# A backward pass of attention and MLP on one core: wq's gradient stored in one piece per block, the held-back stores moved behind the last V load, w2's gradient made first, and w3's gradient shared with ScalarE

## The chip, the cores and the metric

The kernel runs on one core of a Trainium2 chip. The metric is device time in microseconds. Before the change three executions took 749.34, 750.81 and 750.61 us, so the median is 750.61 us. The profiled execution took 750.92 us, of which its instructions span 749.1 us.

## The reference

A decode step with one token. The normalised row goes through attention over a cache of 32 heads with 8192 positions of 128 elements, and through a gated MLP (640 to 1728 to 640), and both are added to the input. The function returns that output and the gradients of eight inputs for a given output gradient.

```python
x = A_x
xn = _layernorm(x, axis=-1)
return x + _A_ref(xn, A_k_cache, A_v_cache, A_wq, A_wo) + _B_ref(xn, B_w1, B_w3, B_w2)
...
_out, _vjp = jax.vjp(_f, A_x, A_k_cache, A_v_cache, A_wq, A_wo, B_w1, B_w3, B_w2)
```

The K and V caches are each 64 MiB in bf16, and so are their gradients: each head loads 2 MiB of K and 2 MiB of V and stores as much in gradients. The gradients of the four attention and MLP weights are outer products of a row and a column: each is made by scaling one vector with a per-partition number.

## The kernel before

One head is one iteration of the main loop over `h`, 32 in all; four heads are a group `g` (eight groups), and two groups are a block `b` of wq (four blocks). In an iteration VectorE makes products of K with q and of V with the output gradient (`product`, L336), TensorE sums them through an identity matrix, and softmax and its gradient follow on small tiles. The gradients of V and K are four tiles `ot` of 1 MiB per head (`outer`): VectorE writes 24 of 32 rows of each (L345), ScalarE the other 8 (L349), and GpSimd's queue stores it (L351). Tiles of `ot` come from a pool of seven buffers; at the start the same seven hold the three parts of w2 (`w2c`), `diag` and `bc_sb`.

All loads go through SyncE's queue (SP) and nearly all stores through GpSimd's queue (POOL). VectorE, ScalarE, SP and POOL run their instructions in the order of the program; TensorE's order is set by the planner that builds the program. A wait at the head of SP or POOL holds all that is queued behind it. K has three buffers, which at the start hold w1, w3 and K of head 0. So `load_k(1)` must wait until the gradient of w1, made in place, has been stored, and `load_k(2)` until that of w3 has.

`mlp_steps` is a generator that is advanced between other pieces of work. Its order before the change: the forward part, `w2_grad(0)`, `dx_part(0)`, `w_grad` of w1; then, outside, `prep_steps(0)` (queries and output gradients of group 0: `qs_g` L258, five copies `woT` L248, `do_g` L274, all ScalarE); then `w2_grad(1)`, `w2_grad(2)`, `dx_part(1)`; the first S products of head 0; `w_grad` of w3; the rest of head 0's preparation. After that come `load_k(1)` and `load_k(2)` and the main loop.

`finish_steps(g)` makes the gradients of wo and wq of a finished group in four pieces, taken at the four calls of `gap()` in the next iteration. When the second group of a block is done it stores the block's wq gradient in five stores, one per 128 rows (`ci`), each behind the ScalarE instruction that makes it. Stores marked `later` go on the list `late`: those of wo of group 6, of wq of block 2 (five), and of wq of group 6. The list is stored at the head of iteration 30 (`h == H - 2`).

Of the kernel before, what the change touches and what calls it, by code (L numbers as in the profile page):

```python
# [11 lines left out]
ALU = mybir.AluOpType  # L12
ACTF = mybir.ActivationFunctionType
# [3 lines left out]
P = 128  # L17
# [4 lines left out]
def kernel(  # L22
# [22 lines left out]
    nc = tc.nc  # L45
    H = A_k_cache.shape[1]
    SK = A_k_cache.shape[2]
    DH = A_k_cache.shape[3]
    D = A_x.shape[2]
    F = B_w1.shape[1]  # L50
    assert DH == P and D % P == 0 and SK % (2 * P) == 0
    NC = D // P
# [4 lines left out]
    NG = H // GH  # L57
    ORDERED = {mybir.EngineType.DVE, mybir.EngineType.SP, mybir.EngineType.Pool, mybir.EngineType.Activation}
    GW = 8
    HB = GW // GH  # L60
# [4 lines left out]
    scale = float(DH) ** -0.5  # L65
# [21 lines left out]
    dwq_v = out_4.rearrange("(p ci) n -> p ci n", ci=NC)  # L87
# [4 lines left out]
    dw1_v = out_6.rearrange("(p ci) f -> p ci f", ci=NC)  # L92
    dw3_v = out_7.rearrange("(p ci) f -> p ci f", ci=NC)
# [3 lines left out]
    with tc.manual_schedule(engines=ORDERED):  # L97
# [8 lines left out]
        def load_k(h):  # L106
            Kt = kpool.tile([P, J, DH], BF16, name="Kt", tag="K")
            nc.sync.dma_start(Kt[:], kc[h])
            kv_tiles[h] = kv_tiles.get(h, [None, None])
            kv_tiles[h][0] = Kt  # L110

        def load_v(h):
            Vt = vpool.tile([P, J, DH], BF16, name="Vt", tag="V")
            nc.sync.dma_start(Vt[:], vc[h])
            kv_tiles[h] = kv_tiles.get(h, [None, None])
            kv_tiles[h][1] = Vt

        grp = {}
        late = []

        def store(dst, src, later=False):
            if later:
                late.append((dst, src))
            else:
                nc.gpsimd.dma_start(dst, src)
# [15 lines left out]
        w1t = kpool.tile([P, NC, F], BF16, name="w1t", tag="K")  # L141
        w3t = kpool.tile([P, NC, F], BF16, name="w3t", tag="K")
# [53 lines left out]
        xn_col = consts.tile([P, NC], F32, name="xn_col")  # L196
        xn_col_bf = consts.tile([P, NC], BF16, name="xn_col_bf")
        xn2 = consts.tile([P, NC, 2], BF16, name="xn2")
# [80 lines left out]
        def finish_steps(g):  # L279
            G_ = grp[g]  # L280
            wo_g = G_["wo"]
            on = small.tile([P, GH], F32, name="on")
            nc.scalar.copy(on[:], G_["on_ps"])
            on_bf = small.tile([P, GH], BF16, name="on_bf")
            nc.scalar.copy(on_bf[:], on[:])
            for r in range(GH):
                for ci in range(NC):
                    nc.tensor.matmul(accbank[:, OUT0 + ci:OUT0 + ci + 1], lhsT=wo_g[:, r, ci * P:(ci + 1) * P],
                                     rhs=on_bf[:, r:r + 1], start=False, stop=True, skip_group_check=True)
            for r in range(GH):  # L290
                nc.scalar.activation(wo_g[:, r, :], g_bc_bf[:], ACTF.Copy, scale=on[:, r:r + 1])
                if r == 1:
                    yield
            store(dwo_v[g], wo_g[:], g == NG - 2)
            yield
            b, k = divmod(g, HB)
            for ci in range(NC):
                nc.scalar.activation(G_["wq"][:, ci, :], G_["dqbc"][:].rearrange("p h d -> p (h d)"),
                                     ACTF.Copy, scale=xn_col[:, ci:ci + 1])
                if g < NG - HB and k == HB - 1:  # L300
                    store(dwq_v[:, ci, b * GW * DH:(b + 1) * GW * DH], G_["wq_all"][:, ci, :], g == NG - HB - 1)
                if ci == 2:
                    yield
            if g >= NG - HB:
                store(dwq_v[:, :, g * GH * DH:(g + 1) * GH * DH], G_["wq"], g < NG - 1)
            grp.pop(g)
# [7 lines left out]
        def new_head(h):  # L314
            st = Head()
            st.g, st.hh = divmod(h, GH)
            st.G = grp[st.g]
            st.K, st.V = kv_tiles.pop(h)
            hs[h] = st
            return st  # L320
# [89 lines left out]
        def keep_wq(st):  # L410
            st.wqT = small.tile([P, D], BF16, name="wqT", bufs=1)
            nc.scalar.copy(st.wqT[:], st.ps_wqT[:])
# [30 lines left out]
        def mlp_steps():  # L443
# [46 lines left out]
            bc_sb = opool.tile([P, 2, F], BF16, name="bc_sb", tag="o")  # L490
            for wi in range(2):
# [4 lines left out]
                for k, b0 in enumerate(range(0, NB, 4)):  # L496
# [6 lines left out]
                    src = bc_ps[:].rearrange("p b a -> p (b a)")[:, 0:cols]  # L503
# [8 lines left out]
            def w2_grad(k):  # L512
                b0, nb, nfull, w2c = w2_parts[k]
                for b, rows in blocks[b0:b0 + nb]:
                    for ci in range(NC):
                        nc.tensor.matmul(accbank[:, OUT0 + ci:OUT0 + ci + 1], lhsT=w2c[0:rows, b - b0, ci * P:(ci + 1) * P],
                                         rhs=hcol_bf[0:rows, b:b + 1], start=False, stop=True, skip_group_check=True)
                    nc.scalar.activation(w2c[0:rows, b - b0, :], g_bc_bf[0:rows, :], ACTF.Copy, scale=hcol[0:rows, b:b + 1])
                nc.gpsimd.dma_start(dw2_v[:, b0:b0 + nfull, :], w2c[:, 0:nfull, :])
                if nfull < nb:  # L520
                    nc.gpsimd.dma_start(out_8[NF * P:F, :], w2c[0:REST, nfull, :])
# [3 lines left out]
            def dx_part(wi, wt):  # L525
                for c0 in range(0, NC, 2):
                    n = min(2, NC - c0)
                    T = tpool.tile([P, n, F], BF16, name="T13", tag="T")
                    nc.vector.tensor_tensor(T[:], wt[:, c0:c0 + n, :],
                                            bc_sb[:, wi, :].unsqueeze(1).to_broadcast([P, n, F]), ALU.mult)  # L530
                    for i in range(F // DR1):
                        nc.tensor.matmul(dx_ps[:, c0:c0 + n, :], lhsT=ident_bf[:], rhs=T[:, :, DR1 * i:DR1 * (i + 1)],  # L532
                                         start=(wi == 0 and i == 0), stop=(wi == 1 and i == F // DR1 - 1),
                                         skip_group_check=True)

            def w_grad(wi, wt, dst):
                nc.vector.tensor_tensor(wt[:].rearrange("p c (a b) -> p c a b", b=2),  # L537
                                        bc_sb[:, wi, :].rearrange("p (a b) -> p a b", b=2).unsqueeze(1)
                                        .to_broadcast([P, NC, F // 2, 2]),
                                        xn2[:].unsqueeze(2).to_broadcast([P, NC, F // 2, 2]), ALU.mult)  # L540
                nc.gpsimd.dma_start(dst, wt[:])

            w2_grad(0)
            dx_part(0, w1t)
            w_grad(0, w1t, dw1_v)
            yield
            w2_grad(1)
            w2_grad(2)
            dx_part(1, w3t)
            yield  # L550
            w_grad(1, w3t, dw3_v)
            yield
            nc.vector.tensor_reduce(dxn_mlp[:], dx_ps[:], AX.X, ALU.add)

# [3 lines left out]
        def gap():  # L558
            if steps and next(steps[0], "end") == "end":
                steps.pop(0)  # L560
# [12 lines left out]
        exps(first)  # L573
        product(first, "DP", 1)
        next(mlp, None)
        load_k(1)
        load_k(2)
        prev = None
        for h in range(H):
            n = new_head(h + 1) if h + 1 < H else None  # L580
            c = hs.pop(h)
            g, hh = divmod(h, GH)
            if h == H - 2:
                for dst, src in late:
                    store(dst, src)
            if n:
                product(n, "S", 0)
            probs(c)
            outer(c, c.do, c.P2, c.Pf, dvc, h, 0)
            if prev:  # L590
                keep_dq(prev)
            gap()
            row_dots(c)
            attend(c)
            turn_wq(c)
            if n:
                product(n, "S", 1)
            outer(c, c.do, c.P2, c.Pf, dvc, h, 1)
            if h + 2 < H:
                load_v(h + 2)  # L600
            gap()
            dscores(c)
            outer(c, c.q, c.U2, c.Uf, dkc, h, 0)
            keep_wq(c)
            if n:
                row_max(n)
                product(n, "DP", 0)
            outer(c, c.q, c.U2, c.Uf, dkc, h, 1)
            if h + 3 < H:
                load_k(h + 3)  # L610
            gap()
            if n:
                exps(n)
                product(n, "DP", 1)
            weights(c)
            gap()
            if hh == 0 and g + 1 < NG:
                if (g + 1) % HB == 0:
                    load_wq((g + 1) // HB)
                load_wo(g + 1)  # L620
            if hh == 1 and g + 1 < NG:
                steps.append(prep_steps(g + 1))
                gap()
            if hh == 2:
                gap()
            prev = c
# [61 lines left out]
```

## Time and profile before

| what | value |
|---|---|
| median of three executions | 750.61 us |
| profiled execution, and its span | 750.92 us, 749.1 us |
| bytes read and written | 151.34 MB and 151.34 MB, 404 GB/s over the span |
| VectorE, TensorE, ScalarE, GpSimd busy | 84%, 73%, 63%, 12% |
| chain that ended last | DMA 61%, VectorE 28%, TensorE 6% |
| five stores of one wq block | 256 KB each, 20.3 us from issue to landing (median) |
| `ot` stores | 128 of 1024 KB, 29.0 us from issue to landing (median) |

The profile shows one execution. In the page's second part the span is cut in 40 slices, and a digit is a busy share in tenths. A row of windows gives, for each engine, the busy time and the instructions in a stretch, then TensorE's granted clock, the share of the 16 DMA engines that was busy, and GB/s. A row of the timeline gives start, duration, engine, line, the tile written and read, and in brackets the idle time before it with what ended it.

### The profile page before, as it was taken

What the parts mean: (1) busy time and instruction counts of PE and PEld (TensorE: products, weight loads), DVE (VectorE), ACT (ScalarE), POOL (GpSimd) and SP (SyncE); (2) the same over time, 40 slices, a digit from 0 to 9 for tenths busy, and PEclk for the clock granted to TensorE, in tenths of its full rate; (3) what the DMA queues carried; (4) which work ended last, traced back from release to release, by engine and by line L of the source; (5) the groups of instructions that cost most, each with busy time, mean ns of one, the idle gap of its engine ahead of it and who ended that gap; (6) DMA issues with size and microseconds to landing.
All of it is one profiled execution on the core that took longest, in us unless ns stands there. A gap on an engine that the chain in (4) does not pass through costs nothing.

```text
span 749.1 us, 15938 instructions
## 1 busy us (share of the span) xinstructions
PE 546.1 (73%) x6513; PEld 323.6 (43%) x6513; DVE 631.8 (84%) x709; ACT 473.3 (63%) x1419; POOL 88.0 (12%) x168
## 2 busy tenths in 40 slices
PE   5677798885868784887778772887787768677860
PEld 3453455452534452444444441444454435344440
DVE  5589999999779985999698993999698998899970
ACT  2453667685658752795666862787555966676772
POOL 0010111010011110111010120111101101101220
PEclk9597779777967887877788887778695989777765
DMA  9978999999999999999999999999999999999796
GB/s 341 415 281 326 421 427 426 422 424 427 425 433 422 422 419 425 426 423 418 431 426 425 425 380 425 426 428 420 429 429 423 429 415 430 427 424 425 311 367 197
DMA packets 37223, 303.71 MB, mean 405 GB/s; under 512 B 4012, under 2 KB 5742, under 8 KB 12062
## 3 DMA queue, kind: packets, MB, share of 16 engines
q0 software_dynamic: 21920, 151.35, 48.8%
q1 hardware_dynamic: 15218, 151.35, 48.5%
q8 instruction: 51, 0.84, 0.4%
q14 instruction: 22, 0.18, 0.1%
q10 hardware_dynamic: 12, 0.00, 0.0%
HBM read 151.34 MB, written 151.34 MB: 404 GB/s over the span
## 4 chain that ended last, share of the span: by engine, by line
DMA 61%; DVE 28%; PE 6%; issue 2%; ACT 1%; SPq 0%; POOL 0%; POOLq 0%; DVEq 0%; ACTq 0%
DMA out_dram<-ot 44%; DVE T L336 12%; DVE ot L345 11%; DMA out_dram<-wo_g 11%; DMA wo_g<-in_A_wo_dram 4%; DMA w3t<-in_B_w_dram 2%; PE psS L338 2%; PE dx_ps L532 1%; DVE S_sb L355 1%; DVE DP_sb L389 1%; DVE w3t L537 1%; PE ps_t L243 1%; PE psDP L338 0%; DVE P L374 0%; ACT woT L248 0%
## 5 line engine op out<-in xcount | busy, mean ns | idle before, releaser
L338 PE MATMUL psDP<-T,ident_bf 128*128 128x512 bf16 x512 | 181.3, 515 | 63.6 <-DVE T L336 63.6
L338 PEld LDWEIGHTS <-ident_bf 128*128 128x128 bf16 x1024 | 119.8, 119 | 213.7 <-issue 157.7
L349 ACT ACTIVATE ot<-qs_g,Uf 128x128 bf16<-128x128 bf16 x512 | 156.4, 389 | 66.5 <-DMA out_dram<-ot 56.4
L349 ACT ACTIVATE ot<-do_g,Pf 128x128 bf16<-128x128 bf16 x512 | 156.3, 389 | 17.7 <-DMA out_dram<-ot 16.8
L336 DVE TENSOR_TENSOR T<-Kt,qs_g 128x4096 bf16<-128x4096 bf16 x64 | 146.4, 2289 | 1.5 <-PE psDP L338 0.7
L338 PE MATMUL psS<-T,ident_bf 128*128 128x512 bf16 x512 | 143.3, 430 | 4.5 <-DVE T L336 4.4
L336 DVE TENSOR_TENSOR T<-Vt,do_g 128x4096 bf16<-128x4096 bf16 x64 | 145.9, 2280 | 0.0
L345 DVE TENSOR_TENSOR ot<-qs_g,U 128x3072 bf16<-128x3072 bf16 x64 | 112.2, 1753 | 38.6 <-DMA out_dram<-ot 38.4
L351 POOL DMA_DIRECT2D out_dram<-ot x128 | 68.2, 533 | 540.0 <-ACT ot L349 204.9
L345 DVE TENSOR_TENSOR ot<-do_g,P 128x3072 bf16<-128x3072 bf16 x64 | 112.3, 1755 | 5.6 <-DMA out_dram<-ot 4.7
L402 PEld LDWEIGHTS <-Kt 128*128 128x128 bf16 x2048 | 57.5, 98 | 13.7 <-issue 11.6
L402 PE MATMUL ob<-U,Kt 128*128 128x1 bf16 x2048 | 57.1, 164 | 3.2 <-DVE U L397 3.1
L382 PEld LDWEIGHTS <-Vt 128*128 128x128 bf16 x2048 | 57.4, 98 | 0.0
L382 PE MATMUL ob<-P,Vt 128*128 128x1 bf16 x2048 | 57.1, 163 | 0.0
L248 ACT COPY woT<-ps_t 128x512 bf16<-128x512 bf16 x40 | 23.0, 576 | 28.8 <-PE ps_t L243 28.6
L368 PEld LDWEIGHTS sm<-rsum,ones_f 128*128 128x128 f32 x64 | 15.8, 271 | 55.5 <-ACT E L367 50.8
L421 ACT ACTIVATE dq_diag<-ident_bf,odq 128x128 bf16<-128x128 bf16 x32 | 12.8, 399 | 40.5 <-DVE odq L417 40.5
L359 PE MATMUL sm<-ident_f,mrow 128*128 128x128 f32 x64 | 18.9, 387 | 26.0 <-DVE mrow L357 26.0
L376 ACT ACTIVATE Pf<-E,rZ 128x16 f32<-128x16 f32 x32 | 9.8, 307 | 38.4 <-DVE rZ L372 38.2
L367 ACT ACTIVATE E<-S_sb,negM 128x64 f32<-128x64 f32 x32 | 11.0, 343 | 33.8 <-DVE negM L364 33.7
L265 PE MATMUL ps_d<-woT,G_rep 128*128 128x512 bf16 x40 | 16.3, 408 | 21.9 <-ACT woT L248 21.7
L243 PE MATMUL ps_t<-ident_bf,wo_g 128*128 128x128 bf16 x160 | 16.9, 233 | 20.2 <-DMA wo_g<-in_A_wo_dram 18.4
(149 smaller groups left out, 522.6 us busy)
## 6 DMA issues: line engine op xcount, KB each, us to landing
out_dram<-ot POOLq DMA_DIRECT2D x128, 1024.0 KB, 29.0
Kt<-in_A_k_cache_dram SPq DMA_DIRECT2D x32, 2048.0 KB, 17.0
Vt<-in_A_v_cache_dram SPq DMA_DIRECT2D x32, 2048.0 KB, 13.9
wq_g<-in_A_wq_dram SPq DMA_DIRECT2D x4, 1280.0 KB, 28.7
wo_g<-in_A_wo_dram SPq DMA_DIRECT2D x8, 640.0 KB, 8.3
out_dram<-wo_g POOLq DMA_DIRECT2D x8, 640.0 KB, 24.3
out_dram<-wq_g POOLq DMA_DIRECT2D x15, 256.0 KB, 20.3
w1t<-in_B_w_dram SPq DMA_DIRECT2D x1, 2160.0 KB, 11.8
```

What stands on the lines that cost most here:

```text
L243: nc.tensor.transpose(ps_t[:, hh * DH:(hh + 1) * DH], wo_g[:, hh, ci * P:(ci + 1) * P], ident_bf[:])
L248: nc.scalar.copy(woT[:], ps_t[:])
L265: nc.tensor.matmul(ps_d[:], lhsT=G_rep[:, ci, :], rhs=woT[:], start=(ci == 0), stop=(ci == NC - 1))
L336: nc.vector.tensor_tensor(T[:], src[:, :, ds_], vec[:, ds_].unsqueeze(1).to_broadcast([P, J, DHH]), ALU.mult)
L338: nc.tensor.matmul(ps[:], lhsT=ident_bf[:], rhs=T[:, :, RUN * i:RUN * (i + 1)], start=(half == 0 and i == 0), stop=(half == 1 and i == DHH ...
L345: nc.vector.tensor_tensor(ot[:, 0:JD], vec.rearrange("p (a b) -> p a b", b=2).unsqueeze(1).to_broadcast([P, JD, DH // 2, 2]), w2[:, j0:j0 ...
L349: nc.scalar.activation(ot[:, j].rearrange("p a b -> p (a b)"), vec, ACTF.Copy, scale=wf[:, half, j - JD:j - JD + 1])
L351: nc.gpsimd.dma_start(dst[h][:, j0:j0 + JH, :], ot[:].rearrange("p j a b -> p j (a b)"))
L359: nc.tensor.matmul(st.sm[:, 8:8 + P], lhsT=mrow[:].to_broadcast([P, P]), rhs=ident_f[:], start=True, stop=True, skip_group_check=True)
L368: nc.tensor.matmul(st.sm[:, 3:4], lhsT=ones_f[:], rhs=rsum[:], start=True, stop=True, skip_group_check=True)
L382: mm = nc.tensor.matmul(st.ob[:, 0:1], lhsT=st.V[:, j, :], rhs=st.P2[:, j, 0:1], start=(j == 0), stop=(j == J - 1), skip_group_check=True)
L402: nc.tensor.matmul(st.ob[:, 1:2], lhsT=st.K[:, j, :], rhs=st.U2[:, j, 0:1], start=(j == 0), stop=(j == J - 1), skip_group_check=True)
```

## The change

Four edits:

- A block's wq gradient goes out in one store of 1280 KB when all five columns are made, in place of five stores of 256 KB.
- The list `late` is stored in iteration 29, right behind `load_v(31)`, in place of the head of iteration 30. It holds three stores in place of seven.
- `w2_grad(1)` moves ahead of `w_grad` of w1 and `w2_grad(2)` right behind it, both ahead of `prep_steps(0)`. `load_k(1)` and `load_k(2)` are called inside `mlp_steps`.
- For w3, ScalarE makes columns 3 and 4 of the gradient (two instructions of 1728 elements) and VectorE's one instruction makes columns 0 to 2.

```diff
             for ci in range(NC):
                 nc.scalar.activation(G_["wq"][:, ci, :], ...)
-                if g < NG - HB and k == HB - 1:
-                    store(dwq_v[:, ci, b * GW * DH:(b + 1) * GW * DH], G_["wq_all"][:, ci, :], g == NG - HB - 1)
                 if ci == 2:
                     yield
+            if g < NG - HB and k == HB - 1:
+                store(dwq_v[:, :, b * GW * DH:(b + 1) * GW * DH], G_["wq_all"][:], g == NG - HB - 1)
...
-            def w_grad(wi, wt, dst):
-                nc.vector.tensor_tensor(wt[:].rearrange("p c (a b) -> p c a b", b=2),
+            def w_grad(wi, wt, dst, nd):
+                for ci in range(nd, NC):
+                    nc.scalar.activation(wt[:, ci, :], bc_sb[:, wi, :], ACTF.Copy, scale=xn_col[:, ci:ci + 1])
+                nc.vector.tensor_tensor(wt[:, 0:nd].rearrange("p c (a b) -> p c a b", b=2),
...
             w2_grad(0)
             dx_part(0, w1t)
-            w_grad(0, w1t, dw1_v)
+            w2_grad(1)
+            w_grad(0, w1t, dw1_v, NC)
+            w2_grad(2)
+            load_k(1)
             yield
-            w2_grad(1)
-            w2_grad(2)
             dx_part(1, w3t)
             yield
-            w_grad(1, w3t, dw3_v)
+            w_grad(1, w3t, dw3_v, NC - 2)
+            load_k(2)
             yield
...
         next(mlp, None)
-        load_k(1)
-        load_k(2)
...
-            if h == H - 2:
-                for dst, src in late:
-                    store(dst, src)
...
             if h + 2 < H:
                 load_v(h + 2)
+            if h == H - 3:
+                for dst, src in late:
+                    store(dst, src)
             gap()
```

More of the change, by code (lines that the diff above doesn't have):

```diff
@@ L534, in dx_part @@
                                          skip_group_check=True)
-            def w_grad(wi, wt, dst):
-                nc.vector.tensor_tensor(wt[:].rearrange("p c (a b) -> p c a b", b=2),
+            def w_grad(wi, wt, dst, nd):
+                for ci in range(nd, NC):
+                    nc.scalar.activation(wt[:, ci, :], bc_sb[:, wi, :], ACTF.Copy, scale=xn_col[:, ci:ci + 1])
+                nc.vector.tensor_tensor(wt[:, 0:nd].rearrange("p c (a b) -> p c a b", b=2),
                                         bc_sb[:, wi, :].rearrange("p (a b) -> p a b", b=2).unsqueeze(1)
-                                        .to_broadcast([P, NC, F // 2, 2]),
-                                        xn2[:].unsqueeze(2).to_broadcast([P, NC, F // 2, 2]), ALU.mult)
+                                        .to_broadcast([P, nd, F // 2, 2]),
+                                        xn2[:, 0:nd].unsqueeze(2).to_broadcast([P, nd, F // 2, 2]), ALU.mult)
                 nc.gpsimd.dma_start(dst, wt[:])
```

## The prediction

> **What bounds the kernel now.** I read the page's slices first, then windows of 2 us over both ends, then the waits of SP, and last the timelines of ScalarE and POOL around the edits. The page:
>
> ```profile
> DMA  9978999999999999999999999999999999999796
> GB/s 341 415 281 326 421 427 426 422 424 427 425 433 422 422 419 425 426 423 418 431 426 425 425 380 425 426 428 420 429 429 423 429 415 430 427 424 425 311 367 197
> ```
>
> From slice 5 to 37 the DMA engines are full at about 425 GB/s; 303.7 MB at that rate are 715 us of the 749. What is left to win is the holes: slices 3 and 4, slice 24, and the end. Windows of the two large ones (last column GB/s):
>
> ```profile
> 42.00:44.00 2.00, 1.28 (x11) 0.64 (x10) 2.00 (x2) 0.95 (x3) 0.55 (x1) 1.00 0.70 281
> ...
> 48.00:50.00 2.00, 1.68 (x31) 1.56 (x29) 1.52 (x2) 2.00 (x3) 0.00 (x0) 1.00 0.09 35
> 50.00:52.00 2.00, 0.92 (x5) 0.45 (x5) 2.00 (x2) 2.00 (x4) 0.14 (x1) 1.00 0.00 0
> ...
> 66.00:68.00 2.00, 2.00 (x11) 0.90 (x10) 1.86 (x4) 0.99 (x4) 0.00 (x0) 1.00 0.35 147
> ...
> 706.00:708.00 2.00, 1.95 (x55) 1.47 (x53) 1.97 (x4) 1.08 (x4) 0.50 (x1) 1.00 0.43 168
> 708.00:710.00 2.00, 0.96 (x21) 0.70 (x19) 1.97 (x4) 2.00 (x7) 0.54 (x1) 1.00 0.13 53
> ```
>
> Summing what the eighteen windows from 40 to 76 lack against 425 gives 4.6 MB, 10.7 us. The seven from 702 to 716 lack 2.8 MB, 6.6 us. SP's waits between 40 and 80 us name the first hole's cause:
>
> ```profile
> SPq L108 <- DMA out_dram<-w1t: 35.0, 1, 35.0
> SPq L108 <- DMA out_dram<-w3t: 16.7, 1, 16.7
> ```
>
> K of head 1 is issued at 51.27, when w1's gradient has landed, and K of head 2 at 68.4, when w3's has. Meanwhile ScalarE (first rows) and POOL (last rows) show w2's stores coming after the first hole:
>
> ```profile
> 31.87 4.42 ACT L518 ACTIVATE w2c<-g_bc_bf,sm_f 128x640 bf16<-128x640 bf16 x6
> 40.66 0.60 ACT L258 ACTIVATE qs_g<-ps_q 128x512 bf16<-128x512 f32 x1 [4.38 <-PE ps_q L253]
> ...
> 47.17 5.84 ACT L518 ACTIVATE w2c<-g_bc_bf,sm_f 128x640 bf16<-128x640 bf16 x8
> ...
> 42.11 0.55 POOL L541 DMA_DIRECT2D out_dram<-w1t  x1 [4.53 <-DVE w1t L537]
> 51.86 1.40 POOL L519 DMA_DIRECT2D out_dram<-w2c  x2 [9.21 <-ACT w2c L518]
> ```
>
> The second hole is of another kind. POOL's rows there:
>
> ```profile
> 705.96 0.54 POOL L125 DMA_DIRECT2D out_dram<-wq_g  x1 [2.28 <-DMA out_dram<-ot]
> 708.71 0.54 POOL L125 DMA_DIRECT2D out_dram<-wo_g  x1 [2.21 <-DMA out_dram<-ot]
> 711.26 0.84 POOL L125 DMA_DIRECT2D out_dram<-wq_g  x1 [2.01 <-DMA out_dram<-ot]
> 714.03 2.48 POOL L351 DMA_DIRECT2D out_dram<-ot  x4 [1.92 <-ACT E L367]
> ```
>
> POOL's stores take eight semaphores in turn, so each waits until the one eight places ahead has landed. Landings keep coming every 2.5 to 2.8 us although 53 GB/s are moved, an eighth of the full rate. So not all 16 engines are at work: one of them is behind. The trace's records of semaphore increments say so: of the sixteen for one store fifteen had come by 706.0 and the last at 714.7, and the last ones follow one another every 2.5 us from 698 to 736. That engine has no hole here; it carries 1 MB of `ot` (64 KB its share) in 2.5 us, as when all run. The hole belongs to the other fifteen.
>
> **The change part by part.**
>
> **w2 first.** Two kinds of cost: ScalarE's order and the DMA queues.
>
> ScalarE: eight instructions of 0.73 us (5.84 / 8) move from 47.17 to 36.29, the end of the first six. There the engine is idle for 4.38 us, which holds six of them; TensorE had read all of w2 by 33.0, so none waits. The other two push `qs_g` and what follows by 1.5 us, `do_g` from 46.12 to 47.6. Head 0's first product on VectorE (48.73) waits for TensorE's sums of w3, which ran behind `ps_d` (last 45.70). At worst it comes 1.5 us later; at best, if the planner puts those sums earlier, VectorE's own gaps of 1.66 and 0.48 us there close and it comes 2.1 earlier.
>
> POOL: the store of w2's second part (0.98 MB) is issued at about 41, ahead of w1's gradient, which is ready at 41.8, so POOL does not hold that up. The queue does: 2.3 us more at 425 GB/s, less what 40 to 44 lacked (0.46 MB, 1.1 us). w1's gradient lands 1.2 us later and SP issues K of head 1 at 52.5. From there to K of head 2 the trace has 17.15 us, in which K (2.10 MB), w2 (1.23) and w3's gradient (2.21) are moved: 13.0 us at 425, and 4.1 of latency and gaps. Without w2 it is 10.1 plus 3.5 to 4.1 (some of the gaps, 0.85 us from 54 to 60, came as w2's stores started). So K of head 2 is issued between 66.1 and 66.7, some 2 us sooner than 68.4.
>
> Behind that point the queues are full until 700, so what the full stretch starts earlier the end is earlier. The other count: 1.23 MB moved into idle DMA time is 2.9 us, the most this part can give; nothing is its least. I take 2.2.
>
> **w3 shared.** VectorE 4.65 us × 3/5 = 2.79, so 1.86 us less on its chain, which is unbroken from 53 to 151. ScalarE's rate from 128 elements (0.306 us, eight of L349 in 2.45) and 640 (0.73): (0.73 − 0.306) / 512 per element, so 1728 take 1.63 us and two take 3.3. They lie in the 8.07 us that ScalarE waits before 61.08, and cost nothing; without that cover they would be 3.3 us on head 0. With the 1.5 us above, w3's gradient is ready at 57.4 at worst, before K of head 1 has gone through (about 59.5). The DMA order so decides, not VectorE: worth 0.3 us, between 0 and 1.
>
> **load_k inside the MLP.** SP has no other DMA between the old place and the new. Both loads wait for the same landings. Nothing.
>
> **One store per block.** Eight POOL instructions of 0.54 us fewer in blocks 0 and 1, beside a POOL busy 12%. A wq store now starts behind the fifth column in place of the first. At slice 24 the five small ones held POOL's eight places with few bytes and the rate was 380; that hole, (425 − 380) × 18.7 us = 0.84 MB or 2.0 us, is of the fifteen engines again. Between 0 and 2.0 gained, and 0.5 lost if the later start leaves a gap. I take 0.
>
> The Trainium skill (DMA: Bandwidth & Descriptors, Anatomy of one DMA) gives each such DMA about 2 us of fixed cost. By it the four fewer at the end would save up to 8 us. Here the slow engine's increments for the five small stores come 0.65 us apart, which is just their bytes: no fixed cost on the path.
>
> **Held-back stores earlier.** 2.62 MB go into POOL's order ahead of head 29's last two `ot`, just behind `load_v(31)` (684.65). The bytes ahead of the slow engine's end are the same; it has work throughout, so it ends when it did. Gained is a bubble of 0.4 us: after the last held-back store, 719.9 in the increments, the next 1 MB took 3.0 us in place of 2.55, as POOL had issued it late. Waiting behind: POOL issues head 29's last two when their places come free, some 7 us later than 690.42 and 695.51, and they land 6.2 us later (2.62 MB / 425). Who waits: VectorE's and ScalarE's tiles of head 31, seven buffers on. The second (718.97) needs what landed at 711.0, the third (721.11) what landed at 713.5: 8.0 and 7.6 us of slack, 1.8 and 1.4 left. Between 0.9 lost and 3.5 gained (rival one); I take 0.4 gained.
>
> The sum against the profiled execution of 750.9: −2.2 − 0.3 − 0 − 0.4 = −2.9, 748.0. The median of the runs is 0.3 below that execution, so 747.7.
>
> [...]
>
> **The rivals.**
>
> One: the end hole fills too. If the fifteen and the one share the work differently once POOL is not stopped by small stores, the end comes as early as the last store allows: issued at 735.16 it landed at 745.8 by the increments; with the least landing time of any `ot` store, 7.1 us, it would be 742.3. So 3.5 us more: 744.2. For it: 53 GB/s at 708. Against it: the increments every 2.5 us.
>
> Two: the gain at the start is eaten. K of head 1 comes 1.2 us later at least; if w1's gradient lands 3 us later, as its last engine was 2.1 us behind the rest already (49.0 and 51.1), and head 0 starts 1.5 later, the full stretch starts where it did, and only the 0.4 at the end is left: 750.2. For it: VectorE's chain from 53 to 151 has no gap. Against: DMA is full there as well.
>
> Three, slower: the held-back stores delay the last head. Stores landed between 7.1 and 39.1 us after issue. If the load of V 31 (2.1 MB, 5 us) goes ahead of them on the slow engine in place of beside them, head 29's tiles land 5 us later than I say, 1.4 to 1.8 of that is slack, and VectorE's last chain and all behind it moves 3.4; with rival two's lost start that is 747.7 + 2.5 + 3.4 = 753.6. It decides from 1.4 us on. For it: head 31's fourth tile already waits for its buffer (to 722.96). Against: before, the same load had landed by 697.6.
>
> **How the numbers follow.** The forecast 0.58 (its own range 746 to 749.1), rival one 0.14, two 0.16, three 0.12. Measured runs spread over 0.2%, 1.5 us, so faster means below 749.1: forecast and rival one, 0.72; the same is rival two, 0.16; slower is three, 0.12. The range from 743.2 (rival one with 1 us of slice 24) to 751.0 leaves out three and the ends of the others.
>
> **What would show it.** Right: two `w2c` groups of ScalarE joined from 31.9 to about 42; 42 to 44 near 400 GB/s; K of head 2 issued near 66.4; `w3t` on VectorE 2.8 us; in the last 50 us three L125 stores ahead of head 29's last `ot`, and still a stretch with less than half the rate. Wrong: no such stretch and an end before 742; SP's first L108 wait ending past 54; VectorE idle for `ot` after 715; slice 24 filled and the time lower by it.

## The result, and the profile after

The changed kernel takes 748.74 us (median of seven; 747.63 to 750.51) against 750.93 us before (median of seven). The two medians are 2.2 us apart. The ratio over all the runs is 0.9978, with a 95% interval from 0.9968 to 0.9988, and this is what the text goes by. Measured once more, with twelve runs, the ratio was 0.9979 (0.9967 to 0.9990). So the kernel is faster by 0.22%, some 1.7 us (0.9 to 2.4), which is just over what a measurement of this kernel can tell from no change. Its profiled execution took 749.1 us, with a span of 747.3 us.

The page of the changed kernel, second part:

```profile
DMA  9988999999999999999999999999999999999993
GB/s 341 413 318 330 405 428 422 423 419 426 425 429 427 422 423 422 426 420 421 431 428 424 424 419 424 408 431 418 431 425 427 427 401 427 426 426 411 414 384 109
```

Three of the holes have changed. Slice 3 went from 281 to 318 GB/s, slice 24 from 380 to 419, and the hole in the third slice from the end (311) has gone. In its place the last slice is emptier: 109 where it was 197. Windows of the changed kernel, with columns as in the prediction:

```profile
42.00:44.00 2.00, 0.31 (x3) 0.28 (x3) 2.00 (x2) 0.97 (x3) 1.66 (x3) 0.74 0.89 330
44.00:46.00 2.00, 2.00 (x14) 1.57 (x12) 1.51 (x1) 0.56 (x1) 0.00 (x0) 0.50 1.18 443
...
50.00:52.00 2.00, 1.90 (x22) 1.63 (x21) 0.47 (x1) 1.50 (x2) 0.00 (x0) 1.00 0.52 167
52.00:54.00 2.00, 1.09 (x24) 0.97 (x22) 1.86 (x1) 2.00 (x3) 0.00 (x0) 1.00 0.25 57
...
66.00:68.00 2.00, 2.00 (x9) 0.81 (x8) 1.89 (x3) 0.21 (x1) 0.00 (x0) 0.78 0.28 57
...
708.00:710.00 2.00, 1.06 (x18) 0.79 (x16) 2.00 (x2) 2.00 (x8) 0.53 (x1) 0.50 1.00 418
...
740.00:742.00 2.00, 0.00 (x0) 0.00 (x0) 0.00 (x0) 0.00 (x0) 0.00 (x0) 0.50 0.06 26
742.00:744.00 2.00, 0.00 (x0) 0.00 (x0) 0.00 (x0) 0.00 (x0) 0.00 (x0) 0.50 0.06 23
```

Two things are to be seen here. At the start the idle stretch of 48 to 54 us did not close; it moved to 50 to 54, and TensorE's granted clock, which was 1.00 from 40 to 58 us before, is 0.50 at 44 us. At the end 708 to 710 is full, but from 738 to 744 the chip moves 23 to 26 GB/s. That is one sixteenth of 425 (26.6): one DMA engine works alone and fifteen are done. The increments say the same. Each of the sixteen engines raises a store's semaphore once when its share has landed, so the sixteenth increment is the last engine's: for the last store fifteen had come by 737.4 us and the sixteenth at 744.2. Before, that last landing was at 745.8.

SP's waits between 40 and 80 us in the changed kernel:

```profile
SPq L108 <- DMA out_dram<-w1t: 36.8, 1, 36.8
SPq L108 <- DMA out_dram<-w3t: 13.5, 1, 13.5
```

K of head 1 is issued at 52.95 us (51.27 before), K of head 2 at 66.9 (68.4 before). The timelines of ScalarE, VectorE and POOL in the changed kernel show the rest of the start:

```profile
31.84 10.18 ACT L518 ACTIVATE w2c<-g_bc_bf,sm_f 128x640 bf16<-128x640 bf16 x14
...
45.44 0.59 ACT L248 COPY woT<-ps_t 128x512 bf16<-128x512 bf16 x1 [2.46 <-PE ps_t L243]
...
51.09 1.32 ACT L274 CAST do_g<-ps_d 128x512 bf16<-128x512 f32 x1 [0.46 <-PE ps_d L265]
52.13 3.35 ACT L538 ACTIVATE w3t<-bc_sb,xn_col 128x1728 bf16<-128x1728 bf16 x2
...
52.14 4.50 DVE L336 TENSOR_TENSOR T<-Kt,qs_g 128x4096 bf16<-128x4096 bf16 x2 [1.67 <-PE dx_ps L532]
56.55 2.85 DVE L539 TENSOR_TENSOR w3t<-bc_sb,xn 128x5184 bf16<-128x5184 bf16 x1
...
40.89 0.84 POOL L519 DMA_DIRECT2D out_dram<-w2c  x1 [3.34 <-ACT w2c L518]
42.07 0.56 POOL L543 DMA_DIRECT2D out_dram<-w1t  x1 [0.34 <-DVE w1t L539]
```

ScalarE's two groups have joined, as the edit says. But head 0's first product starts at 52.14, 3.4 us later than before, because TensorE's transposes (`ps_t`) come late and at half the clock. The row before the change:

```profile
48.73 4.49 DVE L336 TENSOR_TENSOR T<-Kt,qs_g 128x4096 bf16<-128x4096 bf16 x2 [0.48 <-PE dx_ps L532]
```

### The profile page after: what moved, and what is told of

Same layout as the page of the kernel before. It is cut to its first block, busy times and chain, and to the rows that moved or that the text cites. A ratio compares the mean times of both kernels' runs of the same rounds, so it can differ in the third digit from the quotient of the medians.

```text
span 747.3 us, 15903 instructions
## 1 busy us (share of the span) xinstructions
PE 545.3 (73%) x6497; PEld 325.2 (44%) x6513; DVE 630.5 (84%) x709; ACT 476.6 (64%) x1421; POOL 82.7 (11%) x156
## 4 chain that ended last, share of the span: by engine, by line
DMA 66%; DVE 22%; PE 6%; issue 3%; ACT 1%; SPq 0%; POOL 0%; POOLq 0%; DVEq 0%; ACTq 0%
DMA out_dram<-ot 46%; DMA out_dram<-wo_g 11%; DVE T L336 10%; DVE ot L345 7%; DMA wo_g<-in_A_wo_dram 4%; DMA Kt<-in_A_k_cache_dram 3%; DMA w3t<-in_B_w_dram 2%; PE psS L338 2%; PE dx_ps L532 1%; PE psDP L338 1%; DVE S_sb L355 1%; DVE DP_sb L389 1%; PE ps_t L243 1%; DVE T L529 0%; ACT wo_g L291 0%
## 5 line engine op out<-in xcount | busy, mean ns | idle before, releaser
L338 PE MATMUL psDP<-T,ident_bf 128*128 128x512 bf16 x512 | 186.6, 527 | 72.8 <-DVE T L336 72.8
L349 ACT ACTIVATE ot<-do_g,Pf 128x128 bf16<-128x128 bf16 x512 | 156.3, 389 | 15.6 <-DMA out_dram<-ot 14.8
L338 PE MATMUL psS<-T,ident_bf 128*128 128x512 bf16 x512 | 136.5, 415 | 3.5 <-DVE T L336 3.4
L351 POOL DMA_DIRECT2D out_dram<-ot x128 | 68.4, 534 | 574.7 <-ACT ot L349 224.0
L368 PEld LDWEIGHTS sm<-rsum,ones_f 128*128 128x128 f32 x64 | 15.2, 265 | 48.3 <-ACT E L367 43.8
L243 PE MATMUL ps_t<-ident_bf,wo_g 128*128 128x128 bf16 x160 | 18.3, 247 | 17.8 <-DMA wo_g<-in_A_wo_dram 17.7
L355 DVE TENSOR_REDUCE S_sb<-psS 128x64 f32<-128x512 f32 x32 | 21.9, 685 | 9.5 <-PE psS L338 9.5
```

The source lines that it names most:

```text
L243: nc.tensor.transpose(ps_t[:, hh * DH:(hh + 1) * DH], wo_g[:, hh, ci * P:(ci + 1) * P], ident_bf[:])
L338: nc.tensor.matmul(ps[:], lhsT=ident_bf[:], rhs=T[:, :, RUN * i:RUN * (i + 1)], start=(half == 0 and i == 0), stop=(half == 1 and i == DHH ...
L349: nc.scalar.activation(ot[:, j].rearrange("p a b -> p (a b)"), vec, ACTF.Copy, scale=wf[:, half, j - JD:j - JD + 1])
L351: nc.gpsimd.dma_start(dst[h][:, j0:j0 + JH, :], ot[:].rearrange("p j a b -> p j (a b)"))
L355: nc.vector.tensor_reduce(st.S[:], st.ps["S"][:], AX.X, ALU.add)
L368: nc.tensor.matmul(st.sm[:, 3:4], lhsT=ones_f[:], rhs=rsum[:], start=True, stop=True, skip_group_check=True)
```

## The experiments

### Each part by itself

**w2 first.** The kernel before, with w2's order alone:

```diff
             w2_grad(0)
             dx_part(0, w1t)
+            w2_grad(1)
             w_grad(0, w1t, dw1_v)
+            w2_grad(2)
             yield
-            w2_grad(1)
-            w2_grad(2)
             dx_part(1, w3t)
```

> The first part alone: w2's gradient made ahead of w1's store and of the preparation; w3, the wq stores and the held-back stores as before. Theory A (the forecast's: the DMA queues are full from the issue of K of head 2 to the end, so the end moves with that issue): K of head 2 is issued at 66.5 to 67.5 us in place of 68.4 and the time is 1.0 to 2.0 us under the kernel before (ratio 0.9973 to 0.9987). Theory B (the gain of the changed kernel is made at the end; head 0 starts 3.4 us late in it and cancels what the queues win): w3's gradient is ready near 61 in place of 57.8, K of head 2 not before 68.4, ratio 0.9995 to 1.003.

Measured: 0.9996 (0.9984 to 1.0009), that is −0.3 us with an interval from −1.2 to +0.7. Two of its windows, and last the second of them in the kernel before:

```profile
44.00:46.00 2.00, 2.00 (x13) 1.60 (x12) 1.49 (x1) 0.58 (x1) 0.00 (x0) 0.50 1.20 451
...
60.00:62.00 2.00, 0.77 (x2) 0.53 (x3) 1.97 (x4) 0.00 (x0) 0.57 (x1) 0.54 0.33 138
...
60.00:62.00 2.00, 1.10 (x3) 0.41 (x3) 2.00 (x3) 0.44 (x2) 0.00 (x0) 0.50 1.09 454
```

K of head 2 is issued 1.0 us sooner (67.4), but head 0's first product starts at 51.05 (48.73 before), w3's gradient is stored at 60.4 in place of 58.1, and the first `ot` comes at 69.6 in place of 67.3. So the hole has moved: 60 to 62 us carries 138 GB/s where it carried 454. What the largest term of the forecast took for 2.2 us is worth next to nothing here.

**w3 shared.** The kernel before, with ScalarE making columns 3 and 4 of w3's gradient:

```diff
-            def w_grad(wi, wt, dst):
+            def w_grad(wi, wt, dst, nd):
+                for ci in range(nd, NC):
+                    nc.scalar.activation(wt[:, ci, :], bc_sb[:, wi, :], ACTF.Copy, scale=xn_col[:, ci:ci + 1])
...
-            w_grad(1, w3t, dw3_v)
+            w_grad(1, w3t, dw3_v, NC - 2)
```

> The fourth part alone: ScalarE makes columns 3 and 4 of w3's gradient, all else as before. Theory A: VectorE's chain into head 0 is 1.8 us shorter, w3's gradient is ready near 56.0, but its store still stands behind K of head 1 and w2 in the queues, so K of head 2 comes 0 to 1 us earlier: ratio 0.9985 to 1.000. Theory B (VectorE's chain from 53 to 151 us sets the start of the full stretch): the whole 1.8 us, ratio 0.9976.

Measured: 0.9991 (0.9982 to 0.9999), −0.7 us (−1.4 to −0.1). The first `ot` comes at 66.07 us, 1.2 us sooner than before. This edit does what was forecast, at the upper side of its bounds of 0 and 1.

**One store per block.**

```diff
-                if g < NG - HB and k == HB - 1:
-                    store(dwq_v[:, ci, b * GW * DH:(b + 1) * GW * DH], G_["wq_all"][:, ci, :], g == NG - HB - 1)
                 if ci == 2:
                     yield
+            if g < NG - HB and k == HB - 1:
+                store(dwq_v[:, :, b * GW * DH:(b + 1) * GW * DH], G_["wq_all"][:], g == NG - HB - 1)
```

> One store per wq block alone (one for the held-back block too, still stored at the head of iteration 30). Theory A: slice 24 goes from 380 GB/s to about 420, the time stays: ratio 0.9990 to 1.0005. Theory B (a hole filled is time won): 1 to 2 us, ratio 0.9973 to 0.9987.

Measured: 0.9984 (0.9974 to 0.9994), −1.2 us (−2.0 to −0.5). This is the clearest of the single parts, and the forecast had put it at nothing. Slice 24, from 430.7 to 449.4 us, fills (421 GB/s), and slice 38, which holds most of the hole at the end, goes from 311 to 397. From the last increment of the 65th `ot` store to that of the 97th, a stretch that holds slice 24, the kernels with five small stores take 173.7 to 174.2 us (before, w2 first, w3 shared, held-back stores alone), and those with one store take 173.9 to 174.1 (six kernels). So the engine that is behind gains nothing there. From the 97th to the last landing of all, the first take 139.3 to 139.7 us and the others 138.5 to 139.3, 0.7 us less on average. What the traces show of the gain thus lies at the end, where three held-back stores stand in place of seven. By what wait it comes they do not show, and the profiled execution of this kernel took 750.93 us, 0.9 above its own median. That point stays open.

**Held-back stores alone, and both edits of the end together.** The first is the kernel before with this edit; the second has the one store per block as well.

```diff
-            if h == H - 2:
-                for dst, src in late:
-                    store(dst, src)
...
             if h + 2 < H:
                 load_v(h + 2)
+            if h == H - 3:
+                for dst, src in late:
+                    store(dst, src)
```

> The kernel before with the seven held-back stores moved to iteration 29, behind load_v(31), and nothing else. Theory A (one engine sets the end, it has work throughout): only the bubble of 0.4 us goes, ratio 0.9990 to 1.0002, and 704 to 712 still holds a stretch of less than half the rate or shows it at another place near the end. Theory B (the fifteen engines' hole was on the path): 2 to 3.5 us sooner, 0.9950 to 0.9975. Theory C (the held-back stores delay the last head): 1.002 or more.

> One store per wq block and the held-back stores behind the last V load, the start as before. Theory A (one of the sixteen DMA engines is behind and never idle; only its own bubbles can be won): the hole from 702 to 716 us moves behind, the end does not: ratio 0.9990 to 1.0005, and in the last 10 us of the span a stretch near 26 GB/s, a sixteenth of the full rate. Theory B: the end makes most of the changed kernel's gain: ratio 0.997 to 0.9985.

Measured: 0.9999 (0.9989 to 1.0010) for the first, 0.9988 (0.9976 to 0.9999) for both. Windows of 4 us, held-back stores alone:

```profile
698.00:702.00 4.00, 3.12 (x25) 1.57 (x22) 3.86 (x5) 2.61 (x9) 1.00 (x2) 1.00 0.65 263
702.00:706.00 4.00, 3.41 (x73) 2.60 (x74) 3.96 (x5) 2.64 (x10) 0.64 (x2) 1.00 0.60 238
706.00:710.00 4.00, 2.69 (x69) 2.07 (x67) 3.93 (x7) 3.22 (x10) 1.69 (x3) 0.95 0.52 185
```

With five small stores among the seven, the hole is still there, only earlier and flatter, and the time is the same. With one large store in their place it fills wherever the stores stand: slice 38 has 397 GB/s with one store per block alone and 406 with both edits, against 311 before and 291 with the held-back stores moved alone. So it was made by small stores that took POOL's eight places, and the edit of the place does nothing by itself. Theory C, a delay of the last head, falls.

The four single parts add up to −0.3 − 0.7 − 1.2 − 0.1 = −2.3 us. The change as a whole has −1.7 (−2.4 to −0.9), or −1.6 (−2.5 to −0.8) in its second measurement, which the intervals of the parts allow:

> The changed kernel once more, beside the others on the same chip. Ratio to before 0.9968 to 0.9988; if the kernel with w1's store first is really better, this one stands about 0.0013 above it in one and the same call.

Moving the two `load_k` calls was not run by itself. SP, POOL and ScalarE have the same instructions in the same order with and without it, so that it is worth nothing is argued, not measured.

### Why w2 first brought so little

The changed kernel with the last part of w2's gradient moved back behind `prep_steps(0)`, so that ScalarE is free for the preparation sooner:

```diff
             w_grad(0, w1t, dw1_v, NC)
-            w2_grad(2)
             load_k(1)
             yield
+            w2_grad(2)
             dx_part(1, w3t)
```

> The changed kernel with w2's last part (two ScalarE instructions and a store of 240 KB) put back behind the preparation of group 0, so that ScalarE takes up the preparation at about 40.7 us as before the change. Theory A (the part of the start's gain that is missing went because the preparation came late: TensorE had nothing to do from 40 to 43, its granted clock fell to 0.5 from 44 to 50, and head 0's first product came at 52.1 in place of 48.7): the clock stays at 1.00 from 40 to 50, head 0's first product comes at 48.5 to 49.5, w3's gradient is ready near 56, K of head 2 is issued at 65 to 66, and the time is 1 to 2 us under the changed kernel: ratio to the kernel before 0.9950 to 0.9965. Theory B (the queues alone set the end): as the changed kernel, 0.997 to 0.9985.

Measured: 0.9981 (0.9968 to 0.9995), as the changed kernel. `qs_g` is back at 40.61 us, but the clock falls all the same (0.63, 0.50, 0.50 and 0.67 from 42 to 50) and head 0's first product still starts at 51.39. So ScalarE's two extra instructions account for 0.8 of the 3.4 us at most. TensorE's timeline in the changed kernel shows the rest, and its last row is the last group of transposes in the kernel before:

```profile
39.29 0.39 PE L243 MATMUL ps_t<-ident_bf,wo_g 128*128 128x128 bf16 x4
43.69 1.28 PE L532 MATMUL dx_ps<-T,ident_bf 128*128 128x192 bf16 x7 [4.01 <-DVE T L529]
44.77 0.63 PE L243 MATMUL ps_t<-ident_bf,wo_g 128*128 128x128 bf16 x4
...
44.59 0.38 PE L243 MATMUL ps_t<-ident_bf,wo_g 128*128 128x128 bf16 x4 [0.51 <-ACT woT L248]
```

The planner has put sums of w3 (`dx_ps`) ahead of the second group of transposes. They wait 4.01 us for VectorE, which makes w1's gradient until 41.7 us and only then w3's product, and the transposes wait behind them. After that idle time four transposes take 0.63 us in place of 0.39. Before the change all five groups of transposes were done by 45 us. The Trainium skill (TensorE: Matmul & The Clock Gate, Part 1: The HAM clock gate) says that TensorE falls to half its clock after an idle window of about 3.4 us, whose phase runs free; the 4.01 us and the 0.63 against 0.39 agree with it. The kernel with w2's last part later does not fit it as simply. It has no wait that long, and lost the clock too:

```profile
41.24 0.38 PE L243 MATMUL ps_t<-ident_bf,wo_g 128*128 128x128 bf16 x4 [1.72 <-ACT qs_g L258]
43.67 0.64 PE L532 MATMUL dx_ps<-T,ident_bf 128*128 128x192 bf16 x3 [2.05 <-DVE T L529]
```

Here two waits, of 1.72 and 2.05 us with 0.38 us of work between them, were enough.

The next kernel has, beyond that, w1's store ahead of the one of w2's second part, since that store had gone first (40.89 against 42.07) and SP waits for w1's. `w2_grad(1, False)` makes the part without storing it, and `w2_store(1)` issues the store:

```diff
-            w2_grad(1)
+            w2_grad(1, False)
             w_grad(0, w1t, dw1_v, NC)
+            w2_store(1)
```

> As the run before it, and the store of w1's gradient is issued ahead of that of w2's second part, which ScalarE makes when it did. Theory A (K of head 1 waits for w1's landing, so what stands ahead of that store in the queue delays it): K of head 1 is issued at 50.5 to 51.5 in place of 52.9, w2's second part fills the hole behind 50, K of head 2 comes 0.5 to 1.5 us earlier than in the run before it, and the time is as much less: ratio 0.9935 to 0.996. Theory B (what is moved in front of K of head 1 or behind it is the same in bytes): no difference to the run before it, within 0.1%.

Measured: 748.12 us, 0.9965 (0.9951 to 0.9979) against before. Against the kernel just shown, on the same chip, the ratio of medians is 0.9980 (0.9962 to 0.9996, by drawing anew from the twelve runs of each). TensorE's timeline:

```profile
43.62 0.41 PE L537 MATMUL dx_ps<-T,ident_bf 128*128 128x192 bf16 x3 [1.89 <-DVE T L534]
...
44.33 0.39 PE L243 MATMUL ps_t<-ident_bf,wo_g 128*128 128x128 bf16 x4
```

TensorE's longest wait here is 1.89 us, the clock stays at 1.00 from 40 to 58 us, and the transposes take 0.39. K of head 1 is issued at 51.42, K of head 2 at 64.7, and the first product of head 0 starts at 49.37. From 41 us on TensorE runs the same groups in the same order as in the kernel just shown, and up to 43.7 at the same times within 0.1 us. From there the clock makes the difference, and it is worth 2.0 us of head 0's start (51.39 to 49.37). But this start does not always keep the clock. One kernel further down has the same start and differs only in its last eight stores, and in its profiled execution, after waits of 0.99 and 2.21 us, the clock fell:

```profile
44.00:46.00 2.00, 0.96 (x6) 0.66 (x6) 2.00 (x2) 0.00 (x0) 0.81 (x1) 0.81 1.02 415
46.00:48.00 2.00, 2.00 (x15) 1.63 (x14) 0.85 (x1) 0.58 (x1) 0.00 (x0) 0.50 0.77 302
```

So a single profiled execution does not tell how often the clock holds, and the ratio, which goes over all runs, is not parted into what the store's place and what the clock gave. By its ratio this is the fastest of the kernels that do all the work; its interval overlaps that of the changed kernel.

The starts of five kernels stand in one table. The second column is one window from 40 to 70 us. The third works out the difference from before in bytes over 425 GB/s: for the changed kernel (305 − 290) × 30 us = 0.45 MB, 1.1 us. The fourth is the last increment of the 65th `ot` store, in the middle of the kernel. The last three kernels have one store per block too.

| kernel | GB/s, 40 to 70 us | ahead by 70 us | 65th `ot` store landed |
|---|---|---|---|
| before | 290 | 0 | 432.4 us |
| w2 first | 296 | 0.4 us | 432.3 us |
| changed | 305 | 1.1 us | 431.2 us |
| w2's last part later | 312 | 1.6 us | 431.5 us |
| w1's store first | 334 | 3.1 us | 429.5 us |

In these five what is moved by 70 us is kept to the middle of the kernel within 0.7 us. The issue of K of head 2 tells less: it comes 1.0, 1.5, 1.9 and 3.7 us sooner than before in the four, which is 0.2 to 1.0 more than they are ahead at the 65th store. So the count of bytes is the better measure of an edit at the start.

Each row is one execution, and single executions differ at the start: POOL's first store is issued between 36.5 and 36.7 us in these five, and at 37.7 to 38.0 in most others. Among those later ones, three with the changed start have 297 to 299 GB/s and land the 65th store at 431.9 to 432.2 us; three with the start unchanged have 294 to 296 and 432.5 to 433.0. So the 0.4 of w2 first is not clear of what executions differ by, and the changed start is worth between 0.1 and 1.2 us.

### What sets the end

To see whether the stores' bytes on one engine set the end, the changed kernel without the three held-back stores. It leaves 2.62 MB unwritten: wo's gradient of group 6 and wq's of block 2 and group 6.

```diff
-            if h == H - 3:
-                for dst, src in late:
-                    store(dst, src)
```

> The changed kernel without the three held-back stores (the gradients of wo of group 6, of wq of block 2 and of wq of group 6 are not written; 2.62 MB). Theory A (one DMA engine with work throughout sets the end): that engine is done 6.2 us sooner, and the span is shorter by 3.5 us at least (from there the last store itself, made at 733.5, sets the end) and 6.2 at most: ratio to the kernel before 0.989 to 0.994. Theory B (the chain of VectorE and ScalarE to the last store sets the end): nothing, 0.997 to 0.999.

Measured: 0.9919 (0.9898 to 0.9940) against before, 745.23 us. The tail of one engine is gone: the last `ot` store's sixteenth increment comes 0.5 us behind the fifteenth, where it came 7.2 behind in the changed kernel. One window:

```profile
738.00:740.00 2.00, 0.00 (x0) 0.00 (x0) 0.00 (x0) 0.00 (x0) 0.00 (x0) 0.50 0.01 2
```

From the 65th `ot` store to the last it takes 303.9 us, the changed kernel 309.9: 6.0 us less, and 2.62 MB over 425 GB/s are 6.2. By the ratios to before, 0.9919 and 0.9978, the whole kernel is 4.4 us faster than the changed one. So most of these bytes had been on the path, though the page shows them filling holes. That it is not all of them may be due to the last stores, which this kernel waits for: from 730 to 732 us it moves 67 GB/s.

Then the lag itself. With all 128 `ot` stores issued on ScalarE's queue:

```diff
-            nc.gpsimd.dma_start(dst[h][:, j0:j0 + JH, :], ot[:].rearrange("p j a b -> p j (a b)"))
+            nc.scalar.dma_start(dst[h][:, j0:j0 + JH, :], ot[:].rearrange("p j a b -> p j (a b)"))
```

> The changed kernel with the 128 stores of dK and dV issued on ScalarE's queue in place of POOL's; the weights' stores stay on POOL. Theory A (the engine that is behind is so only for stores from POOL's queue: loads from SP's queue show its sixteenth increment 0 to 2 us behind the fifteenth, stores 8 to 19): the sixteenth increment of dK's and dV's stores comes within 2 us of the fifteenth, the last 6 us of the span with 25 GB/s go, and the time falls by 4 to 8 us unless ScalarE's waits for a place in its queue, with loads and stores on one set of eight semaphores, cost more than that. Theory B (that engine is slow whatever the queue): the lag stays at 6 us or more and the time does not fall. By both, the stores ask for places that loads hold, so up to 20 us may be lost by ScalarE's standing still.

Measured: 1.0220 (1.0198 to 1.0241). The sixteenth increment is 0.83 us behind the fifteenth at the median, 1.2 on average and 6.1 at most; in the changed kernel it is 4.5 on average and 15.6 at most, and up to 21.5 in the other kernels with POOL's queue. But the page's row of GB/s shows a new loss:

```profile
GB/s 345 415 306 330 425 428 423 381 388 424 428 420 417 389 428 420 415 395 422 429 423 412 391 421 425 422 415 408 433 420 414 397 424 422 424 421 399 333 241 214
```

Every few slices it falls to 381 to 399, and the tail is longer. VectorE's waits show another one; the two rows below the first are one head's:

```profile
DVE rZ L372 <- PE sm L368: 83.8, 31, 4.5
...
151.85 0.28 PE L368 MATMUL sm<-rsum,ones_f 128*128 128x1 f32 x2
152.17 0.17 DVE L372 RECIPROCAL rZ<-sm 128x1 f32<-128x1 f32 x1 [2.09 <-PE sm L368]
```

The planner has made TensorE's order anew here too. The sum for softmax (L368) stands behind the next sums of `psDP` and `psS`, and VectorE waits for it in 31 of 32 heads, 83.8 us in all. In the kernel before and in the changed one it never does. It waits for `ot` buffers no more (41.2 us in the changed kernel), so what holds VectorE up here is TensorE's order and not the stores. ScalarE stands for more than 1 us before the issue of a store only six times, 17.8 us in all. So this run does not show the queue by itself: DMA is no longer full all the time, and that an engine which is behind catches up in the gaps is left as a rival.

The last two kernels move only the last eight `ot` stores (heads 30 and 31) to SyncE's queue, which has no load left then; one is the changed kernel, the other the one with w1's store first.

```diff
-            nc.gpsimd.dma_start(dst[h][:, j0:j0 + JH, :], ot[:].rearrange("p j a b -> p j (a b)"))
+            eng = nc.sync if h >= H - 2 else nc.gpsimd
+            eng.dma_start(dst[h][:, j0:j0 + JH, :], ot[:].rearrange("p j a b -> p j (a b)"))
```

> The changed kernel with the last eight ot stores (heads 30 and 31) on SyncE's queue. Theory A: lag of the sixteenth increment at the end under 4 us, ratio to before 0.994 to 0.9965. Theory B: lag 6 us or more, ratio 0.997 to 0.999, as the changed kernel.

> The kernel with w1's store ahead of w2's, and in it the last eight ot stores (heads 30 and 31) issued on SyncE's queue in place of GpSimd's. Theory A (the sixteenth engine falls behind only while stores stand on GpSimd's queue): it stops losing from about 697 us on, the sixteenth increment of the last stores is under 4 us late in place of 6 to 10, and the end comes 1 to 3 us sooner than in that kernel: ratio to before 0.992 to 0.995. Theory B (the engine's lag is bytes already queued on it; which queue the last stores take changes nothing): still 6 us late or more, ratio 0.9955 to 0.998.

Measured: 1.0040 (1.0026 to 1.0055) and 1.0023 (1.0011 to 1.0035). Both theories missed: each kernel is slower than the one it was made from, the first by 3.9 us beside the changed kernel on the same chip. The issues and one row of VectorE in the first of them (median us from issue to landing at the end of the first two):

```profile
out_dram<-ot SPq DMA_DIRECT2D x8, 1024.0 KB, 9.7
out_dram<-ot POOLq DMA_DIRECT2D x2, 1024.0 KB, 31.6
```

```profile
729.56 1.76 DVE L345 TENSOR_TENSOR ot<-do_g,P 128x3072 bf16<-128x3072 bf16 x1 [9.07 <-DMA out_dram<-ot]
```

SP's stores are indeed less late: their sixteenth increments come 0.0 to 4.2 us behind. But they overtake what POOL had left on the slow engine. The last two stores of POOL's queue, issued by 701 us, land at 729.5 and 732.0, 18 to 21 us behind their fifteenth increments, and head 31 needs their buffers. VectorE stands for 9.07 us, and from 724 to 730 us the chip moves 25 to 41 GB/s. The Trainium skill (DMA: Bandwidth & Descriptors, Queues, rings and completion order) says that each DMA engine takes the queues it has work for in turn; these landings agree with it. A lag is bytes that stand on one engine, and a second queue does not skip them, it pushes them back.

## Why the prediction was right and wrong

The time, 748.74 us, is 1.0 above the 747.7 forecast and inside its range; 0.3 of that is the median of before, which came out at 750.93 against the 750.61 then known. The sign was right. The gain was put at 2.9 us and measured at 1.7 (0.9 to 2.4). That it is no further off is luck: w2 first was put 1.9 us too high and one store per block 1.2 too low.

- **w2 first: the 2.2 us were mis-sized; alone it gave 0.3 (−0.7 to 1.2), and the start of the changed kernel, with w3 shared, is worth 0.1 to 1.2.** The chain of landings came near to what was worked out: K of head 1 at 52.95 against 52.5, K of head 2 at 66.95 against 66.1 to 66.7 in the changed kernel, but at 67.4 with this part alone. From 42 to 44 us 330 GB/s were moved where near 400 were forecast. What failed is the step "what the full stretch starts earlier the end is earlier", which read the start of the full stretch off K of head 2. With w2's bytes gone from 52 to 66 us, that stretch lacked stores, and `ot` came later than before. Of the bounds by bytes, nothing to 2.9, the lower end was the right one.
- **ScalarE's push: "at worst it comes 1.5 us later" was 3.4.** The working asked only how much later ScalarE would be. TensorE's order, made anew by the planner, put transposes behind sums that wait for VectorE, and the idle time cost the clock. So w3's gradient was ready at 59.4, where 57.4 was the worst forecast.
- **w3 shared: right.** VectorE takes 2.85 us (forecast 2.79), ScalarE's two 3.35 (3.3), and 0.7 us was measured against 0.3, within 0 and 1.
- **load_k: taken at nothing**, since no order on SP, POOL or ScalarE depends on it; no run has it apart.
- **One store per block: taken at 0, measured at 1.2 (0.5 to 2.0).** The bounds, 0.5 lost to 2.0 gained, held it; the value taken did not. The reason given for the zero, that slice 24's hole is of the fifteen engines, agrees with the traces (nothing gained from the 65th to the 97th `ot` store). The working looked at slice 24 alone; the traces have some 0.7 us behind the 97th store, at the end, and the runs don't say by what wait.
- **Held-back stores: the bubble of 0.4 is not to be told from nothing** (−0.1, −0.8 to +0.8). The statement behind it was right: "That engine has no hole here". The hole of the fifteen went where POOL had no small stores, with one store per block the end came sooner by some 0.7 us on average, and the tail of one engine at 26 GB/s is what "a stretch with less than half the rate" had to look like once POOL fed all sixteen in time.
- **Rival one** (the hole fills and the end comes 3.5 us sooner) saw the hole fill, but the end move by some 0.7 on average. Its price was misread as well: 7.1 us is the landing time of w2's first store (36.60 to 43.70), and the least of an `ot` store is 8.9 (714.03 to 722.93), which makes the price 1.8. **Rival two** was half true: most of the start's gain was eaten, as the table shows, though with TensorE's late order in it and not by w1's landing alone. **Rival three** did not come: head 31's fourth tile waited 0.30 us for its buffer and the three before it not at all, so the slack of 1.4 us held.
- **The fixed cost that the Trainium skill gives** (DMA: Bandwidth & Descriptors, Anatomy of one DMA), about 2 us for each DMA, would by estimate have been 8 us for four fewer at the end. The traces do not agree with it there: the two edits of the end together gave 0.9 (0.1 to 1.8).

## What to carry to other kernels

Where DMA is full for most of the time, price an edit at the start by the bytes moved up to the point from which all is full, loads and stores together, and not by when one load is issued; and follow a moved instruction through every engine that a planner may reorder behind it. Here it reordered TensorE at the start of the changed kernel and in the kernel with ScalarE's queue, and both times VectorE came later by it. A hole in the sum of sixteen DMA engines is little to win if one engine is behind: look at the last increment of each store before you count it. Filling such holes gave nothing at slice 24 and some 0.7 us at the end, while 2.62 MB taken away gave 4.4 us. When several small edits are made at once, measure each alone, because a total that agrees can be the sum of terms that do not.

## What the runs showed of the hardware that was not expected

- One DMA engine falls behind on stores from GpSimd's queue: in the changed kernel the sixteenth increment is 0.2 us late at 81 us, 3.0 at 431 and 15.5 at 650, while the sixteenth of K and V loads on SyncE's queue is at most 1.9 late. With the stores on ScalarE's queue it is 1.2 on average, in a kernel whose DMA was not full. The Trainium skill (DMA: Bandwidth & Descriptors, Latency and other measured facts) says that two of the engines are usually slower and guesses at the software queue's descriptor rings; these lags fit a cause in the queue, of one engine, but no run parts the queue from the load on it, and nothing here shows the rings.
- Two queues share the slow engine's time: eight stores on the second queue landed in 9.7 us (median) and held the first queue's two back to 31.6.
- About 4 us of waiting cost TensorE half its clock in a stretch where it was on the path, for 6.8 us in one execution of the changed kernel (0.74, 0.50, 0.50 and 0.55 from 42 to 50 us) and for 3.4 in another (0.60 and 0.55 from 44 to 48). Two waits of 1.72 and 2.05 us, or of 0.99 and 2.21, cost it too; waits of 0.46 and 1.89 did not.
